# Six heads of wo as the moving operand in four column groups, and the second layer norm with one sum product and its rstd behind the first feed-forward product

## The chip, the core and the metric

One Trainium2 chip, one of its cores. The engines that matter here: TensorE (PE; weight loads are listed as PEld), VectorE (DVE), ScalarE (ACT), GpSimd (POOL), and SyncE (SP), which issues nearly all transfers. The metric is the device time of one execution in microseconds; a run's time is a few microseconds longer than the span from its first to its last profiled instruction.

## The reference

A decoding step (one token for each of four sequences) through an adaLN transformer block. Only the parts that the change touches are spelled out.

```
mod = (silu(c) @ w_mod) -> sa, ca, ga, sb, cb, gb           # each 4 x 512
h   = layernorm(x) * (1 + ca) + sa
q   = h @ wq                                                # 32 heads of 128
o   = softmax(q k^T * 128**-0.5) v                          # last 1024 keys of a cache of 8 kv heads
x   = x + ga * (o @ wo)                                     # wo: 4096 x 512
h   = layernorm(x) * (1 + cb) + sb
x   = x + gb * (relu(h @ w1) @ w2)                          # w1: 512 x 1792, w2: 1792 x 512
```

`layernorm(x)` is `(x - mean) / sqrt(var + 1e-5)` over the 512 features, without weights of its own. All inputs and the output are bf16.

## The kernel before

**Layout.** The batch is 4, so activations are kept transposed: features on the 128 partitions, and in the free dimension DT = 4 feature groups times B = 4 sequences (feature d = 4·partition + t). A product with a weight matrix takes a 128x128 block of the weights as the stationary operand and 4 columns of activations as the moving one, with f32 sums in PSUM.

**Order.** TensorE, ACT, DVE and POOL run in the order in which the code is written (a manual schedule). Everything that is large comes in on SP's queue in one fixed order: the first two K tiles, w_mod, wq in two halves, the other K tiles, eight V tiles, wo in five pieces (heads 0-1, 2-3, 4-5, 6, 7; L114), w1 (L120), w2 in three pieces of 512 KB (L128) and one of 256 KB (L129). 32 MB in all. SP waits on earlier landings before it issues further ones; about eight are outstanding. wo takes the buffer of wq, w1 and w2 that of w_mod, V tiles those of K tiles.

**Stages.** Constants on POOL (L133-163); silu and the modulation vectors (L168-244); the first layer norm (L270); q (L277); K transposed on TensorE and scores (L188-291); softmax and the transposed probabilities (L296-336); o (L315); then the part that the change rewrites:

- o is scaled (L357) and regrouped by 16 small products into `o4_ps` (L363), copied to `o4` as bf16 (L366): for l = 0..3 and eight kv heads, 4 columns each. "Heads" are kv heads below: each has 4 blocks l of 128 rows of wo.
- `y_ps` (L373): 8 heads x 4 blocks l x 4 feature groups m = 128 products, stationary a 128x128 block of wo with a column step of 4, moving 4 columns of `o4`. Each head's products wait for its piece of wo.
- `yT` = y times ga (L378), `x1T` = yT + x, written into `xs2` (L379), a zeroed tile in which each sequence has every eighth of 32 columns.
- `layernorm_T` (L246-267), used for both norms: a product with the constant 1/512 gives the sums on all partitions (L248), a reduction the mean (L250), subtraction (L252), square (L254), a second sum product (L256), the variance (L259), Ln and Exp on ACT for 1/sqrt(var + eps) (L261, L263), and three DVE steps to `h2T` (L265-267).
- `x12_ps` (L387): 16 f32 products with the identity bring the residual x back into the output's layout, in four column groups (`tile_position`) of 32 columns. An f32 product is two load-and-multiply pairs in the trace.
- `ffn1` (L397-403) for four groups of m (4, 4, 4, 2): products with w1 (14 x 4), then relu on DVE into `uT32`. `ffn2` (L405-410): 14 x 4 products, stationary 32 columns of `uT32`, moving 128 columns of w2, in four column groups of the output `z_ps`. All of ffn1 stands before ffn2.
- z times gb (L418), plus `x12_ps` (L420), and the store (L421).

In TensorE's order after y: the norm's first sum, its second sum, x12, the first product, the second product.

Of the kernel before, what the change touches and what calls it, by code (L numbers as in the profile page):

```python
# [8 lines left out]
ACT = mybir.ActivationFunctionType  # L9
ALU = mybir.AluOpType  # L10
AX = mybir.AxisListType
bf16 = mybir.dt.bfloat16
f32 = mybir.dt.float32
# [4 lines left out]
def kernel(  # L18
# [14 lines left out]
    nc = tc.nc  # L33
    P = 128
    B, Sq, D = A_x.shape
    _, Hkv, S, Dh = A_k_cache.shape
# [4 lines left out]
    DT = D // P  # L41
    FT = Dff // P
    KT = W // P
    assert Dh == P and B * Hq == P and Sq == 1
    CG = 32
    assert Hkv * rep == CG and B == 4 and rep == 4 and Hkv == 8 and DT == 4 and D == 512
    scale = float(Dh) ** -0.5
    EPS = 1e-5
    HALF = W // 2
    NHW = Hkv // 2  # L50
# [7 lines left out]
    BS = CG // B  # L58
# [3 lines left out]
    const = ctx.enter_context(tc.tile_pool(name="const", bufs=1))  # L62
# [3 lines left out]
    work = ctx.enter_context(tc.tile_pool(name="work", bufs=1))  # L66
    psA = ctx.enter_context(tc.tile_pool(name="psA", bufs=6, space=bass.MemoryType.PSUM))
# [32 lines left out]
    for h in range(Hkv):  # L100
        vt_ = kvpool.tile([P, NI, Dh], bf16, tag="kv", name=f"v{h}")
        nc.sync.dma_start(
            out=vt_[:].rearrange("p j d -> p (j d)"),
            in_=A_v_cache[:, h, S - W:, :].rearrange("b (p j) d -> p b (j d)", j=NI),
# [4 lines left out]
    NL = 4  # L109
    wo_sb = wts.tile([P, Hkv, NL, D], bf16, tag="big", name="wo_sb")  # L110
# [11 lines left out]
    E4 = 4  # L122
# [7 lines left out]
    U_GROUPS = [(m, min(m + E4, FT)) for m in range(0, FT, E4)]  # L130
# [14 lines left out]
    ident_f = const.tile([P, P], f32, name="ident_f")  # L145
    make_identity(nc, ident_f[:])
    onesD = const.tile([P, P], f32, name="onesD")
# [3 lines left out]
    eps_t = const.tile([P, 1], f32, name="eps_t")  # L151
    nc.gpsimd.memset(eps_t[:], EPS)

    QB = 2 * NHW * CG
    QS = QB + rep
    qpad_f = const.tile([P, B * QS], bf16, name="qpad")
    nc.gpsimd.memset(qpad_f[:], 0.0)
    qpad = qpad_f[:, 0:B * QB].rearrange("p (b a h c) -> p b a h c", b=B, a=2, h=NHW)
    qpad_s = qpad_f[:].rearrange("p (b x) -> p b x", b=B)
    uT32 = const.tile([P, FT, CG], bf16, name="uT32")  # L160
    nc.gpsimd.memset(uT32[:], 0.0)
    xs2 = const.tile([P, DT, CG], f32, name="xs2")
# [18 lines left out]
    xT = work.tile([P, DT, B], f32, name="xT")  # L181
# [19 lines left out]
    def k_scores(gi, kT):  # L201
        b, par = gi // 2, gi % 2
        for half in range(2):
            for hw in range(NHW):
# [13 lines left out]
                            axis=AX.XY, op=ALU.add)  # L218
# [5 lines left out]
    for k in range(5):  # L224
        for m in range(DT):
            n0 = k * D + m
            for t in range(DT):
                nc.tensor.matmul(out=mT[:, k, m, :], lhsT=wmod_sb[:, t, n0:(k + 1) * D:DT], rhs=siluT32[:, t, ::BS],  # L228
                                 start=(t == 0), stop=(t == DT - 1))
    gb_ps = psA.tile([NH * CG, DH2], f32, tag="t", name="gb_ps")  # L230
    for t in range(DT):
        for nh in range(NH):
            nc.tensor.matmul(out=gb_ps[nh * CG:(nh + 1) * CG, :], lhsT=siluT32[:, t, :],
                             rhs=wmod_sb[:, t, 5 * D + nh * DH2:5 * D + (nh + 1) * DH2],
                             start=(t == 0), stop=(t == DT - 1), tile_position=(0, nh * CG))
# [4 lines left out]
    sa, ca, ga, sb_, cb = [modT[:, k] for k in range(5)]  # L240
    g1 = work.tile([P, DT, B], f32, name="g1")
    nc.vector.tensor_scalar_add(out=g1[:], in0=ca, scalar1=1.0)
    g2 = work.tile([P, DT, B], f32, name="g2")
    nc.vector.tensor_scalar_add(out=g2[:], in0=cb, scalar1=1.0)

    def layernorm_T(xin, gmul, badd, out_bf, nm):  # L246
        st_ps = psA.tile([P, DT, B], f32, tag="t", name=f"st_ps_{nm}")
        nc.tensor.matmul(out=st_ps[:], lhsT=onesD[:], rhs=xin, start=True, stop=True)  # L248
        mean = work.tile([P, B], f32, name=f"mean_{nm}")
        nc.vector.tensor_reduce(out=mean[:], in_=st_ps[:].rearrange("p t b -> p b t"), axis=AX.X, op=ALU.add)  # L250
        xc = work.tile([P, DT, B], f32, name=f"xc_{nm}")
        nc.vector.tensor_tensor(out=xc[:], in0=xin, in1=mean[:].unsqueeze(1).to_broadcast([P, DT, B]), op=ALU.subtract)  # L252
        sq = work.tile([P, DT, B], f32, name=f"sq_{nm}")
        nc.vector.tensor_tensor(out=sq[:], in0=xc[:], in1=xc[:], op=ALU.mult)  # L254
        st2_ps = psA.tile([P, DT, B], f32, tag="t", name=f"st2_ps_{nm}")
        nc.tensor.matmul(out=st2_ps[:].rearrange("p t b -> p (t b)"), lhsT=onesD[:], rhs=sq[:].rearrange("p t b -> p (t b)"),  # L256
                         start=True, stop=True)
        var = work.tile([P, B], f32, name=f"var_{nm}")
        nc.vector.tensor_reduce(out=var[:], in_=st2_ps[:].rearrange("p t b -> p b t"), axis=AX.X, op=ALU.add)  # L259
        lnv = work.tile([P, B], f32, name=f"lnv_{nm}")  # L260
        nc.scalar.activation(out=lnv[:], in_=var[:], func=ACT.Ln, bias=eps_t[:], scale=1.0)  # L261
        rstd = work.tile([P, B], f32, name=f"rstd_{nm}")
        nc.scalar.activation(out=rstd[:], in_=lnv[:], func=ACT.Exp, scale=-0.5)  # L263
        am = work.tile([P, DT, B], f32, name=f"am_{nm}")
        nc.vector.tensor_tensor(out=am[:], in0=gmul, in1=rstd[:].unsqueeze(1).to_broadcast([P, DT, B]), op=ALU.mult)  # L265
        nc.vector.tensor_tensor(out=xc[:], in0=xc[:], in1=am[:], op=ALU.mult)
        nc.vector.tensor_tensor(out=out_bf, in0=xc[:], in1=badd, op=ALU.add)

    hT = work.tile([P, DT, B], bf16, name="hT")
    layernorm_T(xT[:], g1[:], sa, hT[:], "ln1")  # L270


    qT_ps = psA.tile([P, 2, NHW, rep, B], f32, tag="t", name="qT_ps")
    qT_v = qT_ps[:].rearrange("p a h r b -> p (a h r) b")
    for t in range(DT):
        for hq in range(Hq):
            nc.tensor.matmul(out=qT_v[:, hq, :], lhsT=wq_sb[:, t, hq * Dh:(hq + 1) * Dh], rhs=hT[:, t, :],  # L277
                             start=(t == 0 and hq == 0), stop=(t == DT - 1 and hq == Hq - 1))
    for par in range(2):
        dst = qpad_s[:, :, par * NHW * CG:(par + 1) * NHW * CG].rearrange("p b (h c) -> p b h c", h=NHW)  # L280
        nc.vector.tensor_copy(  # L281
            out=dst[:, :, :, 16 * par:16 * par + rep],
            in_=qT_ps[:, par].rearrange("p h r b -> p b h r"))
# [35 lines left out]
    for iq in range(NQ):  # L319
        ws = slice(iq * WQ, (iq + 1) * WQ)  # L320
        nc.scalar.activation(out=e_sb[:, ws].rearrange("q (u k e) -> q u k e", k=KC, e=2),  # L321
                             in_=sc_ps[:, ws].rearrange("q (u e k) -> q u k e", e=2, k=KC), func=ACT.Exp,
                             bias=nb[:], scale=scale, accum_out=den4[:, iq:iq + 1])
    for iq in range(NQ):
        ws = slice(iq * WQ // 2, (iq + 1) * WQ // 2)
        nc.vector.tensor_tensor(out=p_w[:, ws, :], in0=e_w[:, ws].unsqueeze(2).to_broadcast([P, WQ // 2, B]),  # L326
                                in1=mi4[:].unsqueeze(1).to_broadcast([P, WQ // 2, B]), op=ALU.bitwise_and)
# [21 lines left out]
    for h in range(VEARLY, Hkv):  # L349
        pv(h, 0, NI, last=(h == Hkv - 1))  # L350
        if h == VEARLY:
# [6 lines left out]
                            in0=oT_ps[:].rearrange("p h a b r -> p (h a b r)"), in1=rb[:], op=ALU.mult)  # L358

    o4_ps = psA.tile([P, NL, NHW, 2, B], f32, tag="t", name="o4_ps")  # L360
    for l in range(NL):
        for r in range(rep):
            nc.tensor.matmul(out=o4_ps[r * RB:(r + 1) * RB, l], lhsT=ident_k3[:, l, :], rhs=oT_sb[:, :, :, :, r],  # L363
                             start=True, stop=True, tile_position=(0, r * RB))
    o4 = work.tile([P, NL, NHW, 2, B], bf16, name="o4")
    nc.vector.tensor_copy(out=o4[:].rearrange("p l h a b -> p (l h a b)"), in_=o4_ps[:].rearrange("p l h a b -> p (l h a b)"))  # L366


    y_ps = psA.tile([P, DT, B], f32, tag="t", name="y_ps")
    for h in range(Hkv):  # L370
        for l in range(NL):
            for m in range(DT):
                nc.tensor.matmul(out=y_ps[:, m, :], lhsT=wo_sb[:, h, l, m::DT], rhs=o4[:, l, h % NHW, h // NHW, :],  # L373
                                 start=(h == 0 and l == 0 and m == 0),
                                 stop=(h == Hkv - 1 and l == NL - 1 and m == DT - 1))
    yT = work.tile([P, DT, B], f32, name="yT")
    x1T = xs2[:, :, ::BS]
    nc.vector.tensor_tensor(out=yT[:], in0=y_ps[:], in1=ga, op=ALU.mult)  # L378
    nc.vector.tensor_tensor(out=x1T, in0=yT[:], in1=xT[:], op=ALU.add)  # L379

    h2T = work.tile([P, DT, B], bf16, name="h2T")
    layernorm_T(x1T, g2[:], sb_, h2T[:], "ln2")

    x12_ps = psA.tile([NH * CG, DH2], f32, tag="t", name="x12_ps")
    for g in range(NH):
        for t in range(DT):
            nc.tensor.matmul(out=x12_ps[g * CG:(g + 1) * CG, t::DT], lhsT=xs2[:, t, :],  # L387
                             rhs=ident_f[:, g * (P // NH):(g + 1) * (P // NH)],
                             start=True, stop=True, tile_position=(0, g * CG))

    def w1_cols(t, m):
        f0, e = (m // E4 * E4 * P, E4) if m < FT4 * E4 else (F4, 2)
        return w1_sb[:, t, f0 + m % E4:f0 + e * P:e]
# [1 line left out]
    z_ps = psA.tile([NH * CG, DH2], f32, tag="t", name="z_ps")  # L395

    def ffn1(m0, m1):  # L397
        u_ps = psA.tile([P, m1 - m0, B], f32, tag="t", name=f"u_ps_{m0}")
        for m in range(m0, m1):
            for t in range(DT):  # L400
                nc.tensor.matmul(out=u_ps[:, m - m0, :], lhsT=w1_cols(t, m), rhs=h2T[:, t, :],
                                 start=(t == 0), stop=(t == DT - 1))
        nc.vector.tensor_scalar_max(out=uT32[:, m0:m1, ::BS], in0=u_ps[:], scalar1=0.0)

    def ffn2(m0, m1):  # L405
        for m in range(m0, m1):
# [2 lines left out]
                                 rhs=w2_sb[:, m, nh * DH2:(nh + 1) * DH2],  # L409
                                 start=(m == 0), stop=(m == FT - 1), tile_position=(0, nh * CG))  # L410

    for (m0, m1) in U_GROUPS:
        ffn1(m0, m1)
    for (m0, m1) in U_GROUPS:
        ffn2(m0, m1)
# [36 lines left out]
```

## Time and profile before

| what | us |
|---|---|
| median of 7 runs (86.49 to 88.16) | 87.0 |
| the profiled execution | 86.49 |
| its span, first to last instruction | 84.4 |
| PE busy in the span | 53.5 |
| PEld busy | 46.5 |
| DVE busy | 23.9 |
| ACT busy | 22.7 |
| POOL busy | 3.5 |

The page lists 31.99 MB read from HBM, 379 GB/s over the span, 2492 instructions, of which TensorE has 1134 products and as many loads. A busy TensorE is not one at its peak: products are pipelined and their ends are modelled. In the rows of a view, the first two columns are start and duration in us; in brackets at the end stands the idle time of the engine just before and what ended it ("issue": nothing that the profile shows). In rows of 40 slices a digit is the busy share of 1/40 of the span in tenths, and PEclk is the granted share of TensorE's clock.

### The profile page before, as it was taken

How to read it: one execution, taken by the hardware profiler on the slowest of the kernel's cores; microseconds unless marked ns; L12 is line 12 of the kernel's file. 1: busy time of each engine (PE TensorE's matmuls, PEld its weight loads, DVE VectorE, ACT ScalarE, POOL GpSimd, SP SyncE). 2: the span in 40 equal slices, each digit the busy share in tenths (PEclk: the TensorE clock that was granted, in tenths of full speed). 3: DMA queues.
4: the chain of work that ended last, by engine and by line, in shares of the span. 5: the costliest groups of instructions: out<-in, count | busy, mean ns of one | idle time of the engine just before them, and what ended most of it. 6: DMA issues, size and time to landing. Idle time of an engine off the chain costs nothing.

```text
span 84.4 us, 2492 instructions
## 1 busy us (share of the span) xinstructions
PE 53.5 (63%) x1134; PEld 46.5 (55%) x1134; DVE 23.9 (28%) x64; ACT 22.7 (27%) x35; POOL 3.5 (4%) x17
## 2 busy tenths in 40 slices
PE   0029930596263899999999059985556437578830
PEld 0029920594253649887775059985455436578620
DVE  0024570013300103755456695500011000234120
ACT  2314760001200006977777296010000000020000
POOL 6900000000000000000000000000000000000000
PEclk9999999755555556999999985895555555555555
DMA  0999998999999999999999999999999999999400
GB/s 2 316 423 443 524 408 373 474 388 466 396 400 427 408 427 431 427 411 408 423 431 419 415 419 415 431 415 419 402 400 411 410 427 459 399 384 404 190 0 2
DMA packets 4605, 32.14 MB, mean 381 GB/s; under 512 B 492, under 2 KB 500, under 8 KB 2036
## 3 DMA queue, kind: packets, MB, share of 16 engines
q1 hardware_dynamic: 4580, 31.99, 91.7%
q8 instruction: 8, 0.13, 0.6%
q10 hardware_dynamic: 16, 0.01, 0.1%
q14 instruction: 1, 0.01, 0.0%
HBM read 31.99 MB, written 0.00 MB: 379 GB/s over the span
## 4 chain that ended last, share of the span: by engine, by line
DMA 91%; SPq 2%; PE 1%; issue 1%; DVE 1%
DMA v<-in_A_v_cache_dram 26%; DMA wo_sb<-in_A_wo_dram 24%; DMA wq_sb<-in_A_wq_dram 23%; DMA w<-in_B_w_dram 19%; SPq L82 1%; PE z_ps L408 1%; SPq L91 1%; DVE zg L418 0%; DVE res L420 0%
## 5 line engine op out<-in xcount | busy, mean ns | idle before, releaser
L198 ACT COPY kT<-ktp 128x1024 bf16<-128x1024 bf16 x16 | 15.5, 1015 | 14.8 <-PE ktp L193 13.6
L193 PEld LDWEIGHTS <-k 128*128 128x128 bf16 x256 | 16.7, 108 | 3.5 <-issue 2.5
L193 PE MATMUL ktp<-ident_k,k 128*128 128x128 bf16 x256 | 17.8, 237 | 0.9 <-DMA k<-in_A_k_cache_dram 0.9
L196 DVE COPY kT<-ktp 128x1024 bf16<-128x1024 bf16 x16 | 11.1, 692 | 11.0 <-PE ktp L193 10.7
L315 PE MATMUL oT_ps<-pT,v 128*128 128x16 bf16 x256 | 7.3, 172 | 2.6 <-DMA v<-in_A_v_cache_dram 1.4
L315 PEld LDWEIGHTS <-v 128*128 128x128 bf16 x256 | 7.1, 101 | 2.8 <-DMA v<-in_A_v_cache_dram 1.5
L373 PE MATMUL y_ps<-o,wo_sb 128*128 128x4 bf16 x128 | 5.1, 174 | 4.0 <-DMA wo_sb<-in_A_wo_dram 4.0
L373 PEld LDWEIGHTS <-wo_sb 128*128 128x128 bf16 x128 | 4.7, 118 | 4.4 <-DMA wo_sb<-in_A_wo_dram 4.3
L261 ACT ACTIVATE lnv_ln<-var_ln,eps_t 128x4 f32<-128x4 f32 x2 | 0.6, 298 | 20.6 <-DVE var_ln L259 20.6
L277 PE MATMUL qT_ps<-hT,wq_sb 128*128 128x4 bf16 x128 | 3.7, 166 | 3.8 <-DMA wq_sb<-in_A_wq_dram 2.2
L205 PE MATMUL sc_ps<-kT,qpad 128*32 128x512 bf16 x64 | 5.6, 445 | 0.4 <-DVE qpad L281 0.4
L277 PEld LDWEIGHTS <-wq_sb 128*128 128x128 bf16 x128 | 3.6, 104 | 3.9 <-DMA wq_sb<-in_A_wq_dram 3.9
L228 PE MATMUL mT<-siluT,wmod_sb 128*128 128x4 bf16 x80 | 2.8, 173 | 4.6 <-DMA wmod_sb<-in_w_mod_dram 4.6
L228 PEld LDWEIGHTS <-wmod_sb 128*128 128x128 bf16 x80 | 2.7, 117 | 4.8 <-DMA wmod_sb<-in_w_mod_dram 4.8
L332 PE MATMUL pT_ps<-ident_bf,p_rep 128*128 128x128 bf16 x32 | 3.3, 290 | 2.9 <-DVE p_rep L326 2.9
L332 PEld LDWEIGHTS <-p_rep 128*128 128x128 bf16 x32 | 2.9, 136 | 3.4 <-DVE p_rep L326 3.4
L168 PE MATMUL tp<-ident_bf,cx_sb 8*128 8x8 bf16 x4 | 0.3, 167 | 4.9 <-DMA cx_sb<-in_A_x_dram 4.9
L168 PEld LDWEIGHTS <-cx_sb 8*128 8x128 bf16 x4 | 0.2, 108 | 4.8 <-issue 4.8
L357 DVE TENSOR_TENSOR oT_sb<-oT_ps,rb 128x128 bf16<-128x128 f32 x1 | 0.3, 292 | 8.7 <-PE oT_ps L315 8.7
L326 DVE TENSOR_TENSOR p_rep<-e_sb,mi 128x512 int32<-128x512 int32 x4 | 2.5, 688 | 0.7 <-ACT e_sb L321 0.7
L378 DVE TENSOR_TENSOR yT<-y_ps,modT 128x16 f32<-128x16 f32 x1 | 0.2, 175 | 8.8 <-PE y_ps L373 8.8
L408 PE MATMUL z_ps<-w,uT 128*32 128x128 bf16 x56 | 2.1, 307 | 0.6 <-DMA w<-in_B_w_dram 0.3
(76 smaller groups left out, 37.7 us busy)
## 6 DMA issues: line engine op xcount, KB each, us to landing
k<-in_A_k_cache_dram SPq DMA_DIRECT2D x8, 1024.0 KB, 25.8
v<-in_A_v_cache_dram SPq DMA_DIRECT2D x8, 1024.0 KB, 19.9
wq_sb<-in_A_wq_dram SPq DMA_DIRECT2D x2, 2048.0 KB, 21.4
wmod_sb<-in_w_mod_dram SPq DMA_DIRECT2D x1, 3072.0 KB, 13.7
wo_sb<-in_A_wo_dram SPq DMA_DIRECT2D x3, 1024.0 KB, 20.0
w<-in_B_w_dram SPq DMA_DIRECT2D x1, 1792.0 KB
w<-in_B_w_dram SPq DMA_DIRECT2D x3, 512.0 KB, 17.0
wo_sb<-in_A_wo_dram SPq DMA_DIRECT2D x2, 512.0 KB, 17.6
```

Source lines behind the costliest of these rows:

```text
L82: nc.sync.dma_start(out=kt_[:].rearrange("p j d -> p (j d)"), in_=k_src[b, par, :, S - W:, :].rearrange("h (p j) d -> p h (j d)", j=NI),)
L193: nc.tensor.transpose(out=tp[:, ii, :], in_=k_tiles[gi][:, iq * IQ + ii, :], identity=ident_k)
L196: nc.vector.tensor_copy(out=dst, in_=tp[:])
L198: nc.scalar.copy(out=dst, in_=tp[:])
L205: nc.tensor.matmul(out=sc_ps[hw * CG:(hw + 1) * CG, half * HALF:(half + 1) * HALF], lhsT=qpad[:, b, par, hw, :], rhs=kT[:, half * (NI // 2 ...
L228: nc.tensor.matmul(out=mT[:, k, m, :], lhsT=wmod_sb[:, t, n0:(k + 1) * D:DT], rhs=siluT32[:, t, ::BS], start=(t == 0), stop=(t == DT - 1))
L277: nc.tensor.matmul(out=qT_v[:, hq, :], lhsT=wq_sb[:, t, hq * Dh:(hq + 1) * Dh], rhs=hT[:, t, :], start=(t == 0 and hq == 0), stop=(t == DT ...
L315: nc.tensor.matmul(out=oT_ps[:, hw, par].rearrange("p b r -> p (b r)"), lhsT=v_tiles[h][:, i, :], rhs=pT[:, i, c0:c0 + B * rep], start=(fi ...
L326: nc.vector.tensor_tensor(out=p_w[:, ws, :], in0=e_w[:, ws].unsqueeze(2).to_broadcast([P, WQ // 2, B]), in1=mi4[:].unsqueeze(1).to_broadca ...
L332: nc.tensor.transpose(out=tp[:, ii, :], in_=p_rep[:, i // 2, :, i % 2], identity=ident_bf[:])
L373: nc.tensor.matmul(out=y_ps[:, m, :], lhsT=wo_sb[:, h, l, m::DT], rhs=o4[:, l, h % NHW, h // NHW, :], start=(h == 0 and l == 0 and m == 0) ...
L408: nc.tensor.matmul(out=z_ps[nh * CG:(nh + 1) * CG, :], lhsT=uT32[:, m, :], rhs=w2_sb[:, m, nh * DH2:(nh + 1) * DH2], start=(m == 0), stop= ...
```

## The change

For **wo**, heads 0 to 5 change operands: the stationary operand is 32 columns of `o4` (of which four are used, the others zero), the moving one a row block of wo, 512 columns. The four blocks l go to four column groups of the array, so that `y4_ps` holds four partial sums, each on its own 32 partitions; 24 products in place of 96. DVE and ACT copy half of it each into `y4`, reordered by feature group; four f32 products with the 128x4 selection matrix `sel_b` add up the four partial sums and transpose them into `y_ps`. Heads 6 and 7 follow as before, into the same `y_ps`. `o4` becomes a constant tile, zeroed on POOL ahead of `qpad`, and `sel_b` is made by a DVE reduction of the identity.

For the **second norm**, the sums of s = y·ga + (x - mean of x) and of s² come from one product (32 columns). `ab` holds for each feature group 4 columns of (s - mean)(1 + cb) and 4 columns of sb; the first feed-forward product takes all 8 columns, and its result is put together behind it as u = rstd · (first 4) + (last 4), then relu: three DVE steps where there was one, in two groups of m (8 and 6) instead of four. The residual is written into `xs2` behind `ab`; the variance and rstd follow.

The **first norm** is written out, and multiplies by (1 + ca) before rstd is known.

```diff
@@ constants
+    sel_b = const.tile([P, B], f32, name="sel_b")
+    nc.vector.tensor_reduce(out=sel_b[:], in_=ident_f[:].rearrange("p (l c) -> p c l", c=CG)[:, 0:B, :], axis=AX.X, op=ALU.add)
+    o4 = const.tile([P, NL, NHW, 2, CG], bf16, name="o4")
+    nc.gpsimd.memset(o4[:], 0.0)
+
     QB = 2 * NHW * CG
...
@@ the first norm
-    def layernorm_T(xin, gmul, badd, out_bf, nm):
...
+    def sum_bcast(src, nm):
         st_ps = psA.tile([P, DT, B], f32, tag="t", name=f"st_ps_{nm}")
...
+    mean1 = sum_bcast(xT, "mean")
+    xcen = work.tile([P, DT, B], f32, name="xcen")
+    nc.vector.tensor_tensor(out=xcen[:], in0=xT[:], in1=over_t(mean1[:]), op=ALU.subtract)
...
+    hx = work.tile([P, DT, B], f32, name="hx")
+    nc.vector.tensor_tensor(out=hx[:], in0=xcen[:], in1=g1[:], op=ALU.mult)
+    nc.vector.tensor_tensor(out=hx[:], in0=hx[:], in1=over_t(rstd1[:]), op=ALU.mult)
     hT = work.tile([P, DT, B], bf16, name="hT")
-    layernorm_T(xT[:], g1[:], sa, hT[:], "ln1")
+    nc.vector.tensor_tensor(out=hT[:], in0=hx[:], in1=sa, op=ALU.add)
+
+    ab = work.tile([P, DT, 2, B], bf16, name="ab")
+    nc.vector.tensor_copy(out=ab[:, :, 1, :], in_=sb_)
@@ wo
-    o4 = work.tile([P, NL, NHW, 2, B], bf16, name="o4")
-    nc.vector.tensor_copy(out=o4[:].rearrange("p l h a b -> p (l h a b)"), in_=o4_ps[:].rearrange("p l h a b -> p (l h a b)"))
+    nc.vector.tensor_copy(out=o4[:, :, :, :, 0:B], in_=o4_ps[:])
+
+    HM = 6
+    y4_ps = psA.tile([P, D], f32, tag="t", name="y4_ps")
+    for h in range(HM):
+        for l in range(NL):
+            nc.tensor.matmul(out=y4_ps[l * CG:(l + 1) * CG, :], lhsT=o4[:, l, h % NHW, h // NHW, :], rhs=wo_sb[:, h, l, :],
+                             start=(h == 0), stop=(h == HM - 1), tile_position=(0, l * CG))
+    y4 = work.tile([P, DT, P], f32, name="y4")
+    y4_src = y4_ps[:].rearrange("p (q t) -> p t q", t=DT)
+    nc.vector.tensor_copy(out=y4[:, 0:DT // 2, :], in_=y4_src[:, 0:DT // 2, :])
+    nc.scalar.copy(out=y4[:, DT // 2:DT, :], in_=y4_src[:, DT // 2:DT, :])
     y_ps = psA.tile([P, DT, B], f32, tag="t", name="y_ps")
-    for h in range(Hkv):
+    for t in range(DT):
+        nc.tensor.matmul(out=y_ps[:, t, :], lhsT=y4[:, t, :], rhs=sel_b[:], start=(t == 0), stop=False)
+    for h in range(HM, Hkv):
...
@@ the second norm
-    nc.vector.tensor_tensor(out=x1T, in0=yT[:], in1=xT[:], op=ALU.add)
-
-    h2T = work.tile([P, DT, B], bf16, name="h2T")
-    layernorm_T(x1T, g2[:], sb_, h2T[:], "ln2")
+    s2 = work.tile([P, 2, DT, B], f32, name="s2")
+    nc.vector.tensor_tensor(out=s2[:, 0], in0=yT[:], in1=xcen[:], op=ALU.add)
+    nc.vector.tensor_tensor(out=s2[:, 1], in0=s2[:, 0], in1=s2[:, 0], op=ALU.mult)
+    s2_ps = psA.tile([P, 2, DT, B], f32, tag="t", name="s2_ps")
+    nc.tensor.matmul(out=s2_ps[:].rearrange("p s t b -> p (s t b)"), lhsT=onesD[:], rhs=s2[:].rearrange("p s t b -> p (s t b)"),
+                     start=True, stop=True)
+    me = work.tile([P, 2, B], f32, name="me")
+    nc.vector.tensor_reduce(out=me[:], in_=s2_ps[:].rearrange("p s t b -> p s b t"), axis=AX.X, op=ALU.add)
+    xc2 = work.tile([P, DT, B], f32, name="xc2")
+    nc.vector.tensor_tensor(out=xc2[:], in0=s2[:, 0], in1=over_t(me[:, 0]), op=ALU.subtract)
+    nc.vector.tensor_tensor(out=ab[:, :, 0, :], in0=xc2[:], in1=g2[:], op=ALU.mult)
+    nc.vector.tensor_tensor(out=xs2[:, :, ::BS], in0=yT[:], in1=xT[:], op=ALU.add)
+
+    mm = work.tile([P, B], f32, name="mm")
+    nc.vector.tensor_tensor(out=mm[:], in0=me[:, 0], in1=me[:, 0], op=ALU.mult)
+    rstd2 = work.tile([P, B], f32, name="rstd2")
+    nc.vector.tensor_tensor(out=mm[:], in0=me[:, 1], in1=mm[:], op=ALU.subtract)
+    nc.vector.tensor_scalar_max(out=mm[:], in0=mm[:], scalar1=0.0)
+    nc.scalar.activation(out=mm[:], in_=mm[:], func=ACT.Ln, bias=eps_t[:], scale=1.0)
+    nc.scalar.activation(out=rstd2[:], in_=mm[:], func=ACT.Exp, scale=-0.5)
 
     x12_ps = psA.tile([NH * CG, DH2], f32, tag="t", name="x12_ps")
...
@@ the first feed-forward product
-        u_ps = psA.tile([P, m1 - m0, B], f32, tag="t", name=f"u_ps_{m0}")
+        u_ps = psA.tile([P, m1 - m0, 2, B], f32, tag="t", name=f"u_ps_{m0}")
         for m in range(m0, m1):
             for t in range(DT):
-                nc.tensor.matmul(out=u_ps[:, m - m0, :], lhsT=w1_cols(t, m), rhs=h2T[:, t, :],
-                                 start=(t == 0), stop=(t == DT - 1))
-        nc.vector.tensor_scalar_max(out=uT32[:, m0:m1, ::BS], in0=u_ps[:], scalar1=0.0)
+                nc.tensor.matmul(out=u_ps[:, m - m0].rearrange("p s b -> p (s b)"), lhsT=w1_cols(t, m),
+                                 rhs=ab[:, t].rearrange("p s b -> p (s b)"), start=(t == 0), stop=(t == DT - 1))
+        us = work.tile([P, m1 - m0, B], f32, name=f"us_{m0}")
+        nc.vector.tensor_tensor(out=us[:], in0=u_ps[:, :, 0, :], in1=rstd2[:].unsqueeze(1).to_broadcast([P, m1 - m0, B]),
+                                op=ALU.mult)
+        nc.vector.tensor_tensor(out=us[:], in0=us[:], in1=u_ps[:, :, 1, :], op=ALU.add)
+        nc.vector.tensor_scalar_max(out=uT32[:, m0:m1, ::BS], in0=us[:], scalar1=0.0)
...
-    for (m0, m1) in U_GROUPS:
+    for (m0, m1) in [(0, 2 * E4), (2 * E4, FT)]:
         ffn1(m0, m1)
     for (m0, m1) in U_GROUPS:
         ffn2(m0, m1)
```

More of the change, by code (lines that the diff above doesn't have):

```diff
@@ L244 @@
     nc.vector.tensor_scalar_add(out=g2[:], in0=cb, scalar1=1.0)
-    def layernorm_T(xin, gmul, badd, out_bf, nm):
+    def sum_bcast(src, nm):
         st_ps = psA.tile([P, DT, B], f32, tag="t", name=f"st_ps_{nm}")
[L248 to L256, printed above, removed]
-                         start=True, stop=True)
[L258 to L267, printed above, removed]
@@ new lines, in sum_bcast, with over_t @@
+        nc.tensor.matmul(out=st_ps[:].rearrange("p t b -> p (t b)"), lhsT=onesD[:], rhs=src[:].rearrange("p t b -> p (t b)"),
+                         start=True, stop=True)
+        st = work.tile([P, B], f32, name=f"st_{nm}")
+        nc.vector.tensor_reduce(out=st[:], in_=st_ps[:].rearrange("p t b -> p b t"), axis=AX.X, op=ALU.add)
+        return st
+    def over_t(row):
+        return row.unsqueeze(1).to_broadcast([P, DT, B])
+    mean1 = sum_bcast(xT, "mean")
+    xcen = work.tile([P, DT, B], f32, name="xcen")
@@ new lines @@
+    nc.vector.tensor_tensor(out=xcen[:], in0=xT[:], in1=over_t(mean1[:]), op=ALU.subtract)
+    sq1 = work.tile([P, DT, B], f32, name="sq1")
+    nc.vector.tensor_tensor(out=sq1[:], in0=xcen[:], in1=xcen[:], op=ALU.mult)
+    var1 = sum_bcast(sq1, "var")
+    rstd1 = work.tile([P, B], f32, name="rstd1")
+    lnv1 = work.tile([P, B], f32, name="lnv1")
+    nc.scalar.activation(out=lnv1[:], in_=var1[:], func=ACT.Ln, bias=eps_t[:], scale=1.0)
+    nc.scalar.activation(out=rstd1[:], in_=lnv1[:], func=ACT.Exp, scale=-0.5)
@@ L371 @@
         for l in range(NL):
             for m in range(DT):
-                nc.tensor.matmul(out=y_ps[:, m, :], lhsT=wo_sb[:, h, l, m::DT], rhs=o4[:, l, h % NHW, h // NHW, :],
-                                 start=(h == 0 and l == 0 and m == 0),
-                                 stop=(h == Hkv - 1 and l == NL - 1 and m == DT - 1))
+                nc.tensor.matmul(out=y_ps[:, m, :], lhsT=wo_sb[:, h, l, m::DT], rhs=o4[:, l, h % NHW, h // NHW, 0:B],
+                                 start=False, stop=(h == Hkv - 1 and l == NL - 1 and m == DT - 1))
@@ L376 @@
     yT = work.tile([P, DT, B], f32, name="yT")
-    x1T = xs2[:, :, ::BS]
     nc.vector.tensor_tensor(out=yT[:], in0=y_ps[:], in1=ga, op=ALU.mult)
-    nc.vector.tensor_tensor(out=x1T, in0=yT[:], in1=xT[:], op=ALU.add)
-    h2T = work.tile([P, DT, B], bf16, name="h2T")
-    layernorm_T(x1T, g2[:], sb_, h2T[:], "ln2")
+    s2 = work.tile([P, 2, DT, B], f32, name="s2")
+    nc.vector.tensor_tensor(out=s2[:, 0], in0=yT[:], in1=xcen[:], op=ALU.add)
+    nc.vector.tensor_tensor(out=s2[:, 1], in0=s2[:, 0], in1=s2[:, 0], op=ALU.mult)
```

## The prediction

> **What bounds the kernel now.** I read the page first (slices, then the chain that ended last), then the chain in order of time, the timeline of the last 13 us, and last the idle time that no data explains.
>
> From the page, three rows of the 40 slices and the chain by engine:
> ```profile
> PE   0029930596263899999999059985556437578830
> PEclk9999999755555556999999985895555555555555
> DMA  0999998999999999999999999999999999999400
> ...
> DMA 91%; SPq 2%; PE 1%; issue 1%; DVE 1%
> ```
> The transfers are full from slice 1 to slice 36; 91% of the last chain is transfers. TensorE runs at half clock in everything that the change's main part touches (after 57 us).
>
> The chain in order of time, its end:
> ```profile
> 64.11 15.69 DMA w<-in_B_w_dram
> 79.80 0.04 issue
> 79.84 0.30 PE z_ps L408 x4
> 80.14 0.29 issue
> 80.43 0.75 PE z_ps L408 x20
> 81.18 0.02 issue
> 81.20 0.30 DVE zg L418
> ```
> The third 512 KB piece of w2 lands at 79.80; the last piece (256 KB, issued at 66.66, 13.8 us to landing) at about 80.43. Then come 0.75 us of products, two DVE steps, and the store.
>
> The timeline between wo and w2:
> ```profile
> 69.23 1.96 PE L373 MATMUL y_ps<-o,wo_sb 128*128 128x4 bf16 x48 [1.32 <-DMA wo_sb<-in_A_wo_dram]
> 71.77 0.69 PE L373 MATMUL y_ps<-o,wo_sb 128*128 128x4 bf16 x16 [0.58 <-DMA wo_sb<-in_A_wo_dram]
> 72.50 0.17 DVE L378 TENSOR_TENSOR yT<-y_ps,modT 128x16 f32<-128x16 f32 x1 [8.75 <-PE y_ps L373]
> 73.11 0.58 PE L248 MATMUL st_ps_ln<-xs,onesD 128*128 128x16 f32 x2 [0.65 <-DVE xs L379]
> 74.98 1.36 PE L387 MATMUL x_ps<-ident_f,xs 128*32 128x32 f32 x32
> 76.60 1.95 PE L401 MATMUL u_ps<-h2T,w 128*128 128x4 bf16 x56 [0.26 <-DVE h2T L267]
> 78.48 1.04 PE L408 MATMUL z_ps<-w,uT 128*32 128x128 bf16 x32
> ```
> Between the end of y (72.46) and the first feed-forward product (76.57) lie 4.1 us of norm, but the second product then runs out of w2 at 79.5 and waits. So the 4.1 us do not set the end now: whatever shortens them gains only down to the landing of the last piece.
>
> **A floor and its price.** With everything else ready, the last piece's 8 products (two waves of four; 20 took 0.41 us from first to last start, 0.105 a wave) could start 0.04 us after 80.43 and end at 80.47 + 0.105 + 0.31 (one product) = 80.89, against 81.15 before. So 0.26 us is all that the tail can give while the transfers stand. The change touches no transfer, and SP's queue keeps its order.
>
> **The 0.26 us is an instruction stall.** At 80.14 to 80.43 TensorE waits for nothing in the profile, with its data there for m = 9 to 11. There is one more such stall; these are its row, and what the instruction queue moved before the two (windows 55.55 to 56.7 and 77.9 to 79.1):
> ```profile
> 58.00 2.23 PE L315 MATMUL oT_ps<-pT,v 128*128 128x16 bf16 x78 [1.26 <-issue]
> ```
> ```profile
> q8 instruction: 1, 0.02, 5.5%
> ```
> ```profile
> q8 instruction: 1, 0.02, 5.7%
> ```
> Each stall ends about 1.4 us after such a packet has ended (packets of 1.02 and 1.09 us from 55.60 and 77.98). The page counts 8 of them, 0.13 MB, so 16 KB each. Between the two stalls stand 383 load-and-multiply pairs and three waits of the sequencer, 769 instructions, three times 256 within one. I read it as a block of 256 TensorE instructions arriving late. The Trainium skill (Runtime: NRT & Kernel Launch, Instruction fetch mechanics) has refills of 16 KiB, 256 instructions, and calls the cost of a crossing mostly hidden; by that the stall would be something else and stay, and the sum would be 0. The trace, with 1.26 and 0.29 us of idle TensorE, does not show it hidden.
>
> The change takes 128 pairs of wo down to 24 + 8 (four f32 products are two pairs each, as the norm's is) + 32 = 64, and the norm from 4 pairs to 2: 66 pairs, 132 instructions fewer. The last boundary (pair 1116 of 1134) then lies behind the program's end. The one before it, in the norm's second sum now (74.44), moves to about the 32nd of the first product's 56 pairs, reached near 78.2; its block's packet ran at 67.67, so it is there 8 us early. No stall is left in the tail.
>
> **Part by part: the early edits.** The o4 memset (128x1024, like qpad's 128x1040: 0.96 us) pushes POOL's qpad, uT and xs2 memsets back to 5.2 us; the first reader, the q copy, comes at 28.69. The sel_b reduction waits on DVE for ident_f (2.5 us) while DVE idles until 5.64. The first norm's path to hT loses one 0.2 us DVE step and ab's copy of sb comes behind it; the product there waits until 26.7 us for the second half of wq anyway. All cost nothing; without that cover 1.0, 0.3 and 0.2 us.
>
> **wo, six heads moved (TensorE at half clock).** Heads 4 and 5 start at 69.23 as now. Nearest row for the price: 16 scores products of 128x512 in four column groups took 1.90 us at half clock, one takes 0.63, so a wave of four every 0.42. Eight take 1.05: to 70.28. The copies, 128x256 f32 on DVE and ACT side by side: between 0.29 (128x128 row) and 0.69 (128x1024 bf16 on DVE); between the row of 0.17 for 16 and 0.29 for 128 elements a line gives 0.42, taken: to 70.74 with 0.04 of handover. To TensorE 0.11 (as xs, end 72.97, to 73.08): 70.85. The f32 products by sel_b, 8 pairs: the norm's two loads of at most 0.34 take 0.50 together, so 0.16 a pair; from below 0.035 (x12's 32 in 1.12), from above 0.34. Taken 0.16, the same 128x128 f32 stationary: 1.28, ends 0.3 to 2.7. To 72.13. Heads 6 and 7 have landed by then (71.72): 32 pairs, 1.22 (the row of 32 at 66.69): **73.35, 0.89 later than now.** The new route loses its time behind the last chunk, where the old one was waiting for data.
>
> **The norm.** From y's end: yT 0.04 + 0.28 (start to start, as now), s2 in two steps 0.21 and 0.18, handover 0.11, product and reduction's wait 0.64 as now plus 0.05 for 32 columns instead of 16 (0 to 0.1): reduction at 74.86. Then xc2, ab, xs2 at 0.21 each; xs2 ends at 75.68. **x12 now waits for xs2 and stands on TensorE before the first product.** Today its 1.36 us lie under the variance; now the product waits for them. From 75.79 it ends at 77.15. The Trainium skill (TensorEngine Tiling, Key Properties) says that a change of tiling mode drains TensorE; the trace agrees: after the scores of 128x32 tiles the next full load comes at 30.80, 0.07 before the last product ends. So the first product starts at **77.08 against 76.57**, 0.51 later. w1 has landed by about 76.1 (1792 KB at 512 KB per 1.26 us after 71.72). Ln and Exp of rstd2 (mm's three DVE steps to 76.3, 0.5 on ACT) end by 76.9, ahead of the first use.
>
> **First and second product.** 32 pairs reach DVE 1.24 us after the start (as 76.60 to 77.84): 78.35. Three DVE steps instead of one, 0.22 each: 79.01; second product from 79.12 instead of 78.48. The second half's three steps lie under its first eight m (0.84 us) and end by 79.9. Twelve m at 0.105 bring m = 12 due at 80.38, before the last piece's 80.47. **The landing still sets the end, with 0.09 us to spare.** Sum: end of z 80.89, 0.26 earlier; span 84.4 to 84.14, this execution's time (86.49, 2.09 around its span) to 86.23; against the median of 87.0, 0.51 above this execution, 86.74.
>
> **Rivals.**
> - *Forecast, 0.6:* as above; the norm's gain is eaten by x12 and the detour of y, the landing holds the end, the stall goes. 86.7; its own range with the runs' spread 86.3 to 87.2.
> - *The dependent chain takes over, 0.25 (the slower side):* the f32 products at 0.34 a pair cost 1.4 us more, in front of everything. The end moves one for one once the chain is over 0.09 late; it equals before at 0.35 late and loses 1% at 1.22. At 1.4 late: end of z 82.2, 88.05; halfway, 87.35. For it: only one two-pair burst shows the price. Against it: four moving columns are less than the norm's sixteen.
> - *The stall stays in the tail, 0.1:* if blocks are not counted as I count, 0.29 to 1.26 us come back; the small one gives 87.0, the large one 88.0.
> - *The change moves nothing or shifts transfers, 0.05:* an instruction packet (1.05 us on one engine) now falls near the store. 86.5 to 88.0.
>
> **Range and chances.** About 1%, 0.87 us, is what a measurement of this kernel can tell from no change (its runs span 86.49 to 88.16). The floor lets nothing through that is 1% faster; only the runs' spread does: 0.07. Over 1% slower needs the upper half of the second rival or the third's large stall, with spread 0.14. Range 86.2 (forecast less 0.5 of spread) to 87.7 (the second rival past its middle).
>
> **What would show it.** y ends near 73.3; x12 after xs2 and before the first product, which starts near 77.1; no idle "issue" in z; z waits for w2's last piece near 80.4; last product ends near 80.9. Wrong if the f32 products by sel_b take over 2 us, if z starts after 79.5, or if w2 lands elsewhere.

## The result, and the profile after

The changed kernel takes **86.27 us** (median of 27 runs, 86.01 to 86.47), the one before 86.83 (69 runs, 85.91 to 88.16). The ratio is **0.9957, 95% interval 0.9943 to 0.9972**: about 0.37 us less, 0.24 to 0.49. The forecast was 0.26 less, within 1%; as a time it was 86.74, counted from the 87.0 of seven runs, and 86.27 lies near the low end of its range of 86.2 to 87.7. Some executions of the kernel before, and of the runs with 66 and with 4 extra products below, lie 0.9 us and more above the others; the ratios are meant to leave such disturbed ones out, medians given with a range do not.

The chain that ended last, in order of time, from the changed kernel's profile (86.26 us, span 84.5):

```profile
49.32 20.07 DMA wo_sb<-in_A_wo_dram
69.39 0.04 issue
69.44 1.07 PE y_ps L382 x8
...
77.48 1.17 PE u_ps L438 x32
...
79.49 1.75 PE z_ps L449 x56
81.23 0.02 issue
81.26 0.30 DVE zg L459
```

Before, the chain ran through the transfers up to w2's third piece at 79.80 and had 0.29 us of "issue" inside z. Now it leaves the transfers at wo's third piece (69.39), goes on through the dependent steps, and z's 56 products run in one stretch.

Its timeline in the same stretch (start, duration, engine, line, what; idle time before it):

```profile
69.44 1.05 PE L382 MATMUL y_ps<-wo_sb,o 128*32 128x512 bf16 x8 [1.49 <-DMA wo_sb<-in_A_wo_dram]
...
70.53 0.42 DVE L386 COPY y<-y_ps 128x256 f32<-128x256 f32 x1 [6.61 <-PE y_ps L382]
70.99 0.37 ACT L387 COPY y<-y_ps 128x256 f32<-128x256 f32 x1 [14.73 <-DVE y L386]
...
71.01 1.87 PE L390 MATMUL y_ps<-sel_b,y 128*128 128x4 f32 x8 [0.53 <-DVE y L386]
...
72.73 1.20 PE L394 MATMUL y_ps<-o,wo_sb 128*128 128x4 bf16 x32
...
76.12 1.35 PE L424 MATMUL x_ps<-ident_f,xs 128*32 128x32 f32 x32 [0.80 <-DVE mm L414]
...
77.41 1.97 PE L438 MATMUL u_ps<-ab,w 128*128 128x8 bf16 x56
...
79.49 1.72 PE L449 MATMUL z_ps<-w,uT 128*32 128x128 bf16 x56
```

Every product from y's end on comes later than before: the first feed-forward product at 77.41 against 76.60, z at 79.49 against 78.48. What has become shorter is z itself: 1.72 us in one piece against 2.67 from first to last with two waits. The last landing has not moved earlier: in this execution 80.76, in the one shown of before 80.43. So z ends no earlier here (81.21) than in the profile of before (81.15), a quick execution; the gain shows in the times of many executions, and in how long z ends after the last landing: 0.45 us against 0.72.

### The profile page after: what moved, and what is told of

Same layout as the page of the kernel before. It is cut to its first block, busy times and chain, and to the rows that moved or that the text cites. A ratio compares the mean times of both kernels' runs of the same rounds, so it can differ in the third digit from the quotient of the medians.

```text
span 84.5 us, 2367 instructions
## 1 busy us (share of the span) xinstructions
PE 54.8 (65%) x1068; PEld 46.0 (54%) x1068; DVE 24.8 (29%) x70; ACT 23.1 (27%) x36; POOL 4.4 (5%) x18
## 4 chain that ended last, share of the span: by engine, by line
DMA 78%; PE 11%; DVE 4%; SPq 3%; issue 1%; DVEq 0%
DMA k<-in_A_k_cache_dram 30%; DMA wo_sb<-in_A_wo_dram 24%; DMA v<-in_A_v_cache_dram 24%; PE y_ps L390 2%; PE z_ps L449 2%; PE x_ps L424 2%; SPq L82 1%; PE u_ps L438 1%; PE y_ps L394 1%; PE y_ps L382 1%; SPq L95 1%; PE s_ps L404 1%; SPq L91 1%; DVE y L386 1%; DVE zg L459 0%
## 5 line engine op out<-in xcount | busy, mean ns | idle before, releaser
L198 PEld LDWEIGHTS <-k 128*128 128x128 bf16 x256 | 17.2, 110 | 3.5 <-issue 2.5
L382 PE MATMUL y_ps<-wo_sb,o 128*32 128x512 bf16 x24 | 3.3, 618 | 3.6 <-DMA wo_sb<-in_A_wo_dram 3.6
L382 PEld LDWEIGHTS <-o 128*32 128x32 bf16 x24 | 0.8, 109 | 5.3 <-issue 4.2
L390 PEld LDWEIGHTS y_ps<-sel_b,y 128*128 128x128 f32 x8 | 1.8, 327 | 1.4 <-DVE y L386 1.4
L210 PEld LDWEIGHTS <-qpad 128*32 128x32 bf16 x64 | 1.3, 103 | 2.2 <-DVE qpad L291 0.7
```

The lines of the kernel that those rows point to most:

```text
L198: nc.tensor.transpose(out=tp[:, ii, :], in_=k_tiles[gi][:, iq * IQ + ii, :], identity=ident_k)
L210: nc.tensor.matmul(out=sc_ps[hw * CG:(hw + 1) * CG, half * HALF:(half + 1) * HALF], lhsT=qpad[:, b, par, hw, :], rhs=kT[:, half * (NI // 2 ...
L382: nc.tensor.matmul(out=y4_ps[l * CG:(l + 1) * CG, :], lhsT=o4[:, l, h % NHW, h // NHW, :], rhs=wo_sb[:, h, l, :], start=(h == 0), stop=(h ...
L390: nc.tensor.matmul(out=y_ps[:, t, :], lhsT=y4[:, t, :], rhs=sel_b[:], start=(t == 0), stop=False)
```

## The experiments

**Theory A**: the gain is the instruction stall in z. The block of 256 TensorE instructions that z's tenth m (m = 9) needs comes too late in the kernel before; the change shortens TensorE's program by 132 instructions, so that no block boundary is left there; the landing of w2 holds all else. **Rival B**: the gain is what the change was written for, less work in wo and a shorter norm. **Rival C**: the transfers end earlier. In runs 1 to 5 extra products are put into TensorE's waits for wo; their result is used by nobody.

**1. The kernel before, with more work.**

```diff
+    pad_ps = psS.tile([P, W], f32, tag="s", name="pad_ps")
     for h in range(Hkv):
+        if h in (2, 4):
+            for _ in range(30):
+                nc.tensor.matmul(out=pad_ps[:, 0:B], lhsT=ident_bf[:], rhs=ident_bf[:, 0:B], start=True, stop=True)
```

> The kernel before, with 60 extra products of 128x4 on TensorE, 30 ahead of head 2 and 30 ahead of head 4, where it waits for wo; their result is not used. Theory A (the change's gain is the instruction stall in z, and nothing else): 120 more instructions move the last block boundary from the second product's tenth m into the first product, where its block has long arrived; no idle time with the releaser issue in z, z ends at the landing of the last piece of w2 plus 0.45 us, 0.2 to 0.4 us faster than before (ratio 0.9955 to 0.998). Rival B (the gain comes from the changed wo and norm): more work on TensorE gives no gain, ratio 1.000 or above. Rival C (the change moves the transfers): w2's landing as before, ratio 1.000.

86.22 us (86.05 to 86.37), ratio 0.9955 (0.9929 to 0.9981): the gain of the change without anything of it. The chain of its profile, z's last 24 products:

```profile
79.97 0.04 issue
80.02 0.62 PE z_ps L412 x16
80.64 0.02 issue
80.65 0.43 PE z_ps L412 x8
```

m = 8 starts 0.04 after the third piece's landing, m = 9 to 11 follow without a break, and m = 12 starts 0.04 after the last landing (80.61). So the gain needs none of the work that B puts it down to. The last landing is no earlier than before either, against C. The extra products did not raise the clock: TensorE's granted share is 0.50 from 60 to 82 us here as in the kernel before.

**2. The changed kernel, made as long as before.** 33 such products ahead of head 2 and 33 ahead of head 4, in the loop of the wide products.

```diff
     for h in range(HM):
+        if h in (2, 4):
+            for _ in range(33):
...
```

> The changed kernel with 66 extra products of 128x4 in the waits ahead of heads 2 and 4, so that its TensorE program is as long as that of before and the block boundary falls on the second norm's product and 256 instructions later in z. Theory A: the boundary is crossed near 74.7 us, its block comes 6.0 us later (80.7, as 74.44 to 80.43 before), and TensorE needs it near 80.45: an idle time of 0.2 to 0.6 us with the releaser issue in z, and 0.2 to 0.4 us more than the changed kernel (86.5 to 86.7 us, ratio to before 0.998 to 1.001). Rival B and rival C: as the changed kernel, 86.27 us, ratio 0.9957.

Ratio 1.0016 (0.9977 to 1.0056): the gain is gone. The median is 86.98 over times from 86.04 to 88.09. The profiled execution was one of the quick ones, 86.27, and has no stall, against what was expected of it. A second execution was profiled:

> A second profile of the changed kernel with 66 extra products, to see an execution of it. Theory A: where the block's packet starts over 3 us after the crossing at 74.7 us, z shows an idle time with the releaser issue between m = 8 and m = 10, which ends 1.2 to 1.5 us after the packet has ended; where it starts earlier, none.

86.86 us, span 84.8. The timeline:

```profile
79.50 2.03 PE L453 MATMUL z_ps<-w,uT 128*32 128x128 bf16 x56
...
80.80 0.46 PEld L453 LDWEIGHTS <-uT 128*32 128x32 bf16 x19 [0.32 <-issue]
```

56 products take 2.03 us instead of 1.72, with the weight loads idle for 0.32 before 80.80; that load is TensorE's 1116th, as the stalled one of the kernel before was. The last piece of w2 had landed at 80.67. In the profile of before the stall ends just at the last landing, 80.43, and could be taken for a wait for it; here it ends 0.13 after that, and in runs 1 and 5 m = 9 to 11 do not wait for it.

**3. The same with six products more.** 72 instead of 66.

```diff
-            for _ in range(33):
+            for _ in range(36):
```

> The changed kernel with 72 extra products in the waits ahead of heads 2 and 4, six more than the run with 66. Theory A in its narrow form: the crossing moves from the norm's sum product (74.7 us) into the products of head 7 before it, the block comes early enough, and the time is that of the changed kernel, 86.2 to 86.35 us, ratio 0.995 to 0.997, although there is more work than with 66. If the extra products themselves cost the time that 66 of them cost: 86.9 to 87.1 us, ratio 1.000 to 1.003.

86.28 us (86.16 to 86.39), ratio 0.9911 (0.9878 to 0.9944), and z in one stretch of 1.68 us. The ratio is below the expected 0.995 to 0.997, but the time is as expected and that of the changed kernel; with 86.78, the median of before beside it without the disturbed executions, it gives 0.994. So it was not the extra work that cost time in run 2; where the boundaries fall decides.

**4. and 5. Few products in the kernel before.** First 4, then 12, all ahead of head 2.

```diff
+        if h == 2:
+            for _ in range(4):
...
```

> The kernel before with 4 extra products of 128x4 ahead of head 2, where TensorE waits for wo; their result is not used. Theory A in its narrow form: the block that z needs is asked for when TensorE's sequencer crosses the boundary before it, which stands in the norm's second sum behind a wait of the sequencer (74.4 us). Eight instructions more move that crossing into head 7's products, before 72 us, so the block is there by 78.5 at the latest, and z does not stall: ratio 0.9955, as with 60 extra products. If only the boundary's place in z mattered (it moves by four products, from m = 9 to m = 8), the stall would stay: ratio 0.998 to 1.002. Rivals B and C: 1.000.

Inconclusive as a time: ratio 0.9978 (0.9927 to 1.0030), five of twelve times at 86.16 to 86.27 and seven at 87.28 to 87.71. The chain of the profiled execution, one of the seven (the third piece of w2 landed at 79.89):

```profile
79.89 0.70 issue
80.59 0.85 PE z_ps L412 x24
```

The stall now stands at the start of m = 8, four products earlier in z, again at TensorE's 1116th load, and ends 0.07 after the last landing (80.52). The narrow form of the theory was wrong in this run: it had the block asked for as the boundary is crossed, and 4 products should have been enough.

```diff
-            for _ in range(4):
+            for _ in range(12):
```

> The kernel before with 12 extra products ahead of head 2 instead of 4. With 4, some executions kept the stall; in the one profiled, the block's packet started at 78.06, 3.53 us after the wait of TensorE's sequencer at 74.5 us, as in the kernel before (3.54 us after 74.44). Theory A, corrected: the block is asked for a few instructions behind the boundary, so 4 products left the request behind that wait; 12 bring it into head 7's products, before 73 us. No execution stalls in z: packet before 77, no idle time with the releaser issue in z, 86.15 to 86.35 us with no time above 86.5. If the stall came from something else that a few products only shake: times spread as with 4 (86.2 to 87.7).

86.09 us (85.98 to 86.36), ratio **0.9944** (0.9917 to 0.9971), and none of its twelve times above 86.4; the median is a little under the 86.15 expected. That the request stands a few instructions behind the boundary fits 4 and 12 products; nothing between them was run. Timeline of z:

```profile
78.65 1.05 PE L412 MATMUL z_ps<-w,uT 128*32 128x128 bf16 x32
80.09 1.03 PE L412 MATMUL z_ps<-w,uT 128*32 128x128 bf16 x24 [0.40 <-DMA w<-in_B_w_dram]
```

Twelve useless products in a wait for wo do as much for this kernel as the whole change.

**6. The change's norm alone**, with wo as before: 2 load-and-multiply pairs less than before. Against the changed kernel:

```diff
-    HM = 6
-    y4_ps = psA.tile([P, D], f32, tag="t", name="y4_ps")
...
+    for h in range(Hkv):
+        for l in range(NL):
+            for m in range(DT):
+                nc.tensor.matmul(out=y_ps[:, m, :], lhsT=wo_sb[:, h, l, m::DT], rhs=o4[:, l, h % NHW, h // NHW, :],
```

> The kernel before with the two norms and the first feed-forward product of the change, and wo as before (128 products with wo stationary). TensorE has 2 load-and-multiply pairs less than before, so the block boundary stays in z. Theory A: the stall in z stays, ratio 0.998 to 1.001 although the first product starts about 0.3 us earlier (w1 has landed by 76.0 to 76.3). Rival B: the shorter norm brings the gain, ratio 0.9957 or below.

86.68 us (86.12 to 87.05), ratio 1.0007 (0.9973 to 1.0041): no gain. Its first profile (86.29) has no stall in z, against what was expected; a second execution:

> A second look at the kernel with the new norm alone. Theory A: an idle time with the releaser issue between m = 8 and m = 10 where the packet starts after about 77.7 us (it ends about 2.4 us behind that start), none where it starts earlier; the time goes with it, about 86.2 us without and 86.6 to 87.0 with.

```profile
79.98 0.40 PE L432 MATMUL z_ps<-w,uT 128*32 128x128 bf16 x7 [0.59 <-DMA w<-in_B_w_dram]
80.84 0.72 PE L432 MATMUL z_ps<-w,uT 128*32 128x128 bf16 x17 [0.46 <-issue]
```

86.76 us, with 0.46 of idle "issue" inside m = 9, at the 1116th load once more, and 0.28 after the last landing (80.56). The expectation that the time goes with it held: 86.29 and 86.76.

**7. The change's wo alone**, with the old norm. Against the kernel before:

```diff
-    for h in range(Hkv):
+    for h in range(HM):
+        for l in range(NL):
+            nc.tensor.matmul(out=y4_ps[l * CG:(l + 1) * CG, :], lhsT=o4[:, l, h % NHW, h // NHW, :], rhs=wo_sb[:, h, l, :],
...
+    for t in range(DT):
+        nc.tensor.matmul(out=y_ps[:, t, :], lhsT=y4[:, t, :], rhs=sel_b[:], start=(t == 0), stop=False)
+    for h in range(HM, Hkv):
```

> The kernel before with the change's wo alone (six heads moving, y4, sel_b) and the old norm and first product. TensorE has 64 load-and-multiply pairs less, so no block boundary is left in z. Theory A with the detour's price: no idle time with the releaser issue in z, but y ends near 74.0 as in the changed kernel, the norm before it takes 4.1 us, the first product starts near 78.0, z near 79.95 and runs 1.74 us without waiting: z ends near 81.7, 0.4 to 0.5 us later than in the changed kernel, 86.6 to 86.8 us, ratio 0.998 to 1.002. If the landing of w2 alone set the end: 86.2, ratio 0.9955. Rival B (fewer and wider products on wo bring the gain): 0.9957 or below.

86.79 us (86.52 to 86.84), ratio 1.0011 (0.9986 to 1.0036). The chain:

```profile
78.13 1.94 PE u_ps L418 x56
80.08 1.64 PE z_ps L425 x56
81.72 0.02 issue
```

z in one stretch, no stall, and yet no gain: the first product starts at 78.13, z runs past the landing and ends 0.5 us later than in the changed kernel. The detour over y4 takes back what the missing stall gives; in the whole change the shorter norm returns it.

**8. x12 back under the norm.** In the changed kernel the residual is written ahead of the sum product, and x12 follows that product.

```diff
+    nc.vector.tensor_tensor(out=xs2[:, :, ::BS], in0=yT[:], in1=xT[:], op=ALU.add)
     s2_ps = psA.tile([P, 2, DT, B], f32, tag="t", name="s2_ps")
...
+    x12_ps = psA.tile([NH * CG, DH2], f32, tag="t", name="x12_ps")
+    for g in range(NH):
...
     me = work.tile([P, 2, B], f32, name="me")
...
-    nc.vector.tensor_tensor(out=xs2[:, :, ::BS], in0=yT[:], in1=xT[:], op=ALU.add)
```

> The changed kernel with the residual written to xs2 ahead of the norm's sum product and x12's 16 products right behind that product, under the norm's DVE steps. By the prediction's step (x12 stands in front of the first product) the first product starts 0.8 to 1.0 us earlier, near 76.5, and z near 78.6. Theory A with the landing as floor: z then waits for w2 and the time falls by 0 to 0.25 us only (86.0 to 86.3). Rival B (the dependent chain sets the end): 0.8 to 1.0 us less, 85.3 to 85.5.

86.16 us (86.05 to 86.28), ratio 0.9955 (0.9924 to 0.9985), as the changed kernel. The timeline:

```profile
75.20 1.36 PE L410 MATMUL x_ps<-ident_f,xs 128*32 128x32 f32 x32
76.49 1.98 PE L438 MATMUL u_ps<-ab,w 128*128 128x8 bf16 x56
78.56 1.05 PE L449 MATMUL z_ps<-w,uT 128*32 128x128 bf16 x32
80.07 1.03 PE L449 MATMUL z_ps<-w,uT 128*32 128x128 bf16 x24 [0.46 <-DMA w<-in_B_w_dram]
```

The first product comes 0.92 us earlier, and nearly all of it turns into a wait for w2. This is the floor: 0.9 us less on the dependent chain are worth about 0.1.

**When the block comes.** From the packet records of the instruction queue (q8): start and end of the last packet before z's boundary, and what z then did.

| profiled execution | packet, us | z resumes, after packet's end | idle "issue" in z |
|---|---|---|---|
| before | 77.98 to 79.06 | 80.43, 1.37 | 0.29 |
| before, 4 extra | 78.06 to 79.17 | 80.59, 1.42 | 0.70 |
| changed, 66 extra, second execution | 78.24 to 79.32 | 80.80, 1.48 | 0.32 |
| norm alone, second execution | 78.49 to 79.55 | 80.84, 1.28 | 0.46 |
| changed, 66 extra, first | 76.41 to 77.48 | no stall | 0 |
| norm alone, first | 76.93 to 78.01 | no stall | 0 |
| changed, 72 extra | 76.34 to 77.42 | no stall | 0 |
| before, 12 extra | 74.26 to 75.32 | no stall | 0 |
| before, 60 extra | 73.72 to 74.74 | no stall | 0 |

A packet that ends by 78.0 is in time, one that ends after 79.0 is not. The same program can have either (66 extra: 76.41 and 78.24; norm alone: 76.93 and 78.49), which fits that the times of these kernels spread and those of the changed one (86.01 to 86.47) hardly do. Why the packet comes early or late is open.

The length of a block can be read from where TensorE idles with "issue" inside dense products: at its 734th load in every profile, at the 862nd with the norm alone (first execution; first line below), at the 990th with 60 extra products (second line), and at the 1116th in z:

```profile
65.19 1.13 PE L378 MATMUL y_ps<-o,wo_sb 128*128 128x4 bf16 x30 [0.48 <-issue]
...
70.07 1.53 PE L377 MATMUL y_ps<-o,wo_sb 128*128 128x4 bf16 x42 [0.29 <-issue]
```

These loads are 128, 128 and 126 load-and-multiply pairs apart, about 256 instructions each, and every such stall ends 1.2 to 1.6 us after a 16 KB packet has ended.

None of the versions is clearly faster than the change: 86.09 with 12 extra products in the kernel before, 86.16 with x12 early and 86.28 with 72 extra have intervals that overlap the change's.

## Why the prediction was right

*The floor and the stall.* The step that carried the forecast, 0.26 us of instruction stall against a landing that does not move, is what runs 1, 2, 3 and 5 show. Counting instructions in blocks of 256 told from the profile of before that the change would take the boundary out of z. (Between the two stalls of before stand 382 pairs and not 383; with three waits 767 instructions, still within one of three blocks.) What the prediction had from one execution, 0.29 us, is a quantity that varies: 47 executions of before beside runs 1 to 8, without the disturbed ones, have spans from 84.3 to 84.9 with a median of 84.6, against 84.4 for the changed kernel. Ten of them, at 86.06 to 86.29, are as quick as the changed kernel.

*The size.* Only 0.2 of the 0.37 us lie in the span, so the 0.26 were a fair size for it, but not, as the prediction had it, all that the tail can give. The other 0.2 lie around the span: 2.07 us between span and time in the median of those executions of before (1.75 to 1.89 in the ten quick ones), 1.84 in the changed kernel. The prediction kept 2.09 for both; this term of its sum was wrong, by as much as the rest of the gain. Runs without a stall in z have 1.78 to 1.88, also wo alone with its longer span; the norm alone, with the stall, 1.94, and 66 extra products 2.04. So it goes with the boundary in z; by what mechanism stays open.

*wo.* The eight f32 products are the term that was mis-sized: 0.16 us a pair was taken from the norm's burst of two. The first two of the eight loads do start 0.17 apart, but the others 0.21: 1.87 us in all with the last product's 0.35, 1.72 instead of 1.28 up to head 6's first product. The waves of wide products (1.05) and the copy (0.42) came as estimated. The copies did not run side by side, as the prediction had them: ACT started when DVE had written (70.99, released by DVE). It cost nothing, since the first f32 products need DVE's half only.

*Norm and x12.* x12 stands in front of the first product as foreseen, 1.29 us from its start to that product's, the 1.36 less 0.07 of the sum. From y's end to x12 it was 2.19 instead of 2.44: half of the difference is that xs2 does not wait for ab, and DVE starts such a step 0.09 after the one before it, not 0.21. So this error and that of the f32 products, 0.44 too little, partly cancel, which is luck; z began at 79.49 instead of 79.12, 0.2 of it because wo's third piece landed later in this execution (its first products start at 69.44 against 69.23).

*Landing against chain.* The prediction had the chain 0.09 ahead of the landing, and z waiting for w2's last piece. In the profile z waits for nothing: m = 12 comes due at 79.49 + 12 x 0.105 = 80.75, and the last piece landed at 80.76. In the profiles of runs 2 (first execution) and 3 z began at 79.44 and 79.51 and the landings were at 80.56 and 80.64, so there the chain was late by 0.14 and 0.13. The margin was not there, then, and the end is a tie, give or take 0.1. Of the signs that the prediction named, z's start of 79.49 is a hair short of the 79.5 that would have meant wrong, and w2's last piece landed 0.33 later than in the one execution that the sum was worked out from (80.52 to 80.76 in the eleven other profiles), so the last product ended at 81.21 and not near 80.9. Run 8 frees the chain and the landing holds; run 7 delays z by 0.5 and the time follows. Both halves of the tie are shown.

*Rivals.* The dependent chain took over by 0.1 us at most; alone with the old norm it does so by 0.5 (run 7). The stall did not stay, and the transfers kept their order and did not end earlier.

*The early edits* left no trace: q's products still wait for wq's second half, until 26.6 us.

*What a crossing costs.* Where the next block comes late, TensorE idles for 0.29 to 0.70 us in z, and for 0.9 to 1.5 us under the attention's products, where a wait for v follows and covers it. The Trainium skill (Runtime: NRT & Kernel Launch, Instruction fetch mechanics) calls the cost of crossing a 16 KiB boundary mostly hidden. It was hidden at the crossings without a stall, and these runs show that it need not be.

## What to carry to other kernels

An engine that idles with its data there and nothing to wait for ("issue"), hundreds of instructions into a dense stretch, may be short of instructions: look for the instruction queue's packets, find the period between two such idles, and work out where the next boundaries fall, before crediting a gain to the edit that moved them. A control that only shifts the program (a dozen idle products in an existing wait) tells the two apart, and here is worth as much as the edit. Where the last transfer's landing is the floor, work out first what the tail behind it can give.

## What the runs showed of the hardware that was not expected

- An instruction packet of 16 KB takes 0.9 to 1.1 us while the weights are coming in, and where TensorE waits for it, it resumes only 1.2 to 1.6 us after the packet's end. From the wait that held the program just at the boundary (74.44 and 74.7) to the packet's start it was 3.5 us in two executions and 1.8 in a third, of the same program as the second.
- The dense products of the attention stall in every profile at the same load (the 734th), for 0.9 to 1.5 us.
- f32 products of 128x128 with 4 moving columns: 0.21 us a pair from start to start at half clock, against 0.033 for bf16 ones.
- The time around the span is not a constant of a kernel: 1.75 to 2.12 us in 45 of those 47 executions of the kernel before.
